# Eight moves in a fused two-branch kernel: a fold's evictions, two scaled tiles of C, half-tiles of the state, and three loads

## The chip, the cores and the metric

The kernel runs on one core of one Trainium2 chip. The core has five engines that run their own instruction streams in order and meet at semaphores: PE (TensorE, the matmuls; its weight loads are shown as PEld), DVE (VectorE), ACT (ScalarE), POOL (GpSimd, used here almost only to issue transfers that add to their target) and SP (SyncE, which issues the other transfers). The metric is device time in microseconds (us) of one execution. A profile of one execution gives, for every instruction, start, duration and what ended the wait before it. All times below count from the start of that profiled span.

## The reference

The inputs are a sequence x of 2048 rows by 1024 channels, and the weights of two branches whose results are mixed row by row with a gate g:

```python
g = _sigmoid((x * gate_w).sum(-1, keepdims=True))
a = _A_ref(x, ...)      # diagonal complex state space model
b = _B_ref(x, k, v, ...)  # gated long convolution
return g * a + (1 - g) * b
```

Branch a keeps 1024 complex states. With `Lam_bar = exp(dt * Lam)` and `B_bar = ((Lam_bar - 1) / Lam) * B` it computes `Bu = x B_bar^T`, runs `h = Lam_bar * h + Bu[t]` over all 2048 rows, and gives `y = 2 Re(h C^T) + x * Dskip`. Branch b filters k with four taps per channel, multiplies by v to get kv, convolves kv over the sequence with a kernel `ssm_k` of full length 2048 per channel (in the reference by an FFT of length 4096), adds `kv * ssm_D`, and multiplies by q, which is x itself here. Types are bfloat16 in and out.

## The kernel before

The kernel is written as one long function in which every engine's instructions are issued in the order of the code (helper `put`, line 92: all compute goes through it, which is why nearly every row of the profile is at L94). Python generators stand for pieces of work; `step(gen)` issues the piece up to the next `yield`, `run(gen)` the rest. So the order of `step` and `run` calls is a schedule written out by hand, and moving one call moves instructions on several engines at once. PSUM is one pool of four 4 KB tiles (`ps2`, line 86); a matmul group can begin only when one of the four has been evicted by ACT or DVE.

The work has three stages.

**Start (to about 60 us).** Angles of a table are reduced on DVE and turned into cosines and sines on ACT: `SF` and `CF` for the forward transform, then `SI` and `CI` for the inverse one from `inverse_angles` (line 360: two ACTIVATEs `h<-row`, then two DVE instructions) and `inverse_table`. `first_times_v` (line 537) makes the first channel block's taps, multiplies them by v and mirrors them (`ev`, `ks`). `fold_K(c)` (line 462) folds the long kernel of block c: ten matmuls into two PSUM tiles `foldk`, each evicted by ACT into `eok`. `fwd_K` and `fwd_V` multiply by the tables; their PSUM tiles are `psk` and `psv`.

**Convolution (the loop at line 1070 over c = 0 to 6, and the block after it for c = 7).** Channels go in 8 blocks of 128. In an iteration the engines work on different blocks: `inverse(c - 1)` (line 677) multiplies the product spectrum G by CI and SI (tiles `psz`, 8 matmuls each, evicted into `cv` and stored to DRAM by SP), `times_v` on block c + 1, `products(c)` (line 625) on DVE, which ends with G, and `fwd_K`, `fwd_V` of block c + 1. Between them stand `step(parts)`: a third of a tile of the state branch's Bu. `Bu_tile` (line 774) has three steps: 16 matmuls into `odd` with its eviction into U, 16 matmuls into `even`, and 8 short matmuls `even<-U,lamd` with the eviction `U<-even`. Between the second and the third step the `even` tile stays in PSUM. The input of a later part of the state branch, block 2 of x (`xT`, loaded by SP with a transposing transfer), goes into the memory that v2 holds, so that its load waits for the last `ks<-ks,v` on DVE.

**State branch (line 1188 on).** `Bu_plain` gives tiles `both` (16 matmuls, two evictions). `turn_C(pi)` (line 1199) multiplies the complex tile pi of C by a complex factor per state: two ACTIVATEs write `m`, two more multiplications scale the tile in place, and `m` is added, for pi 0, 1, 4 and 5 by a POOL transfer that adds (`gather`), for the others by DVE. `turn_U` (line 815) makes ACT write Q and POOL add it to U. Then a loop over j = 0 to 15 runs one DVE scan per j (`scan`, line 834), and matmuls `Bu_next` or `psy` (`Cy_row`, `Cy_group`) as `plan` says (line 1308: for j = 3 it is "B12 B13 C0"). `scale_b(t)` (line 941) is two ACTIVATEs on the convolution's row t (`pbb`, read back from DRAM) and on D times the gate (`gd<-rows`), and a POOL transfer that adds them. For scans 4, 12, 13 and 14 the products `Q<-hb,lam` are made by ACT when the list `put_off` is called, and DVE adds them to U in the next scan. `scale_a` evicts a `psy` tile, `combine` adds to it, `store` writes rows out.

Of the kernel before, what the change touches and what calls it, by code (L numbers as in the profile page):

```python
# [9 lines left out]
ALU = mybir.AluOpType  # L10
# [10 lines left out]
def kernel(  # L21
# [440 lines left out]
    def fold_K(c):  # L462

        kb = lds.pop(("kn", c)).rearrange("p (a f) d -> p a f d", f=4)
        eo = eos["k", c] = eo_pool.tile([128, 2, 2, 4, 128], BF16, name="eok")
        for mt in range(2):
            ps = ps2([128, 2, 4, 128], "foldk")
            for e in range(2):
                mm(ps[:, e], ident, kb[:, :, 2 + mt], True, False)
                mm(ps[:, e], refl[:, e], kb[:, :, 1 - mt], False, mt == 0)  # L470
                if mt == 1:

                    mm(ps[:, e, 0], refl[0:1, e], sD[:, c * 128:(c + 1) * 128], False, True)
            act(eo[:, :, mt], ps, func=ACT.Copy)
            yield
# [355 lines left out]
    put_off = []  # L831
# [175 lines left out]
    def step(gen):  # L1007
        next(gen, None)

    def run(gen):  # L1010
        for _ in gen:
            pass

    def steps(gen, n):
        for _ in range(n):
            step(gen)
# [12 lines left out]
    act(flat(CF), flat(hf), func=ACT.Sin, bias=pih, scale=-TWO_PI)  # L1029
    angles = inverse_angles()  # L1030
    turns = inverse_table()
    step(angles)
    step(first)
    step(first)
    run(fold_K(0))
    ts(NCF, CF, -1.0, None, ALU.mult)
    step(angles)
    run(first)
    run(angles)
    load("kT", 1)  # L1040
# [29 lines left out]
    for c in range(NC - 1):  # L1070
# [38 lines left out]
        tabs, back, prod = turn_table(c - 1) if c <= NG else none, inverse(c - 1), products(c)  # L1109
        step(old)  # L1110
        step(tabs)
        step(back)
        step(tv)
        steps(prod, 3)
# [4 lines left out]
        run(old)  # L1119
        if nn < NC:  # L1120
            dg = dgs(nn)
        if c in (2, 6):
            step(parts)
        fwd_K(n, (0, 1))
        if c in (2, 6):
# [48 lines left out]
            run(next(tiles))  # L1174
            run(next(tiles))
        fwd_V(n, (0, 1))
        if c < 6:
            step(parts)
            if c in (1, 3):
                step(parts)  # L1180
        fwd_V(n, (2, 3))
        if c == 5:
            step(parts)
        if c == 1:
            lam_diag(1, lam_pool)
# [13 lines left out]
    def turn_C(pi):  # L1199
        by_sum = pi in (0, 1, 4, 5)  # L1200
        if pi in (4, 5):
            m = [s5p["Q"].tile([128, D], BF16, name="Q") for c in range(2)]
        else:
            whole_m = m_pool.tile([128, 2, D], BF16, name="m")
            m = [whole_m[:, c] for c in range(2)]
        for c in range(2):
            act(m[c], CT[pi][:, 1 - c], func=ACT.Identity, scale=mc2i[:, pi:pi + 1])
            yield
        for c, f in enumerate((c2r, mc2r)):
            ts(CT[pi][:, c], CT[pi][:, c], f[:, pi:pi + 1], None, ALU.mult)  # L1210
            if by_sum:
                gather(CT[pi][:, c], m[c])
        if not by_sum:
            tt(CT[pi], CT[pi], whole_m, ALU.add)
# [7 lines left out]
    with tc.tile_pool(name="fin", bufs=1, side="right") as fin:  # L1222

        count = iter(range(16))

        def room(shape, dt, name):
            return fin.tile(shape, dt, name=name, tag=f"fin{next(count)}")

        prod, back = products(c, 0, room, False), inverse(c - 1)
        run(old)  # L1230
        steps(prod, 3)
        run(next(tiles))
        steps(turning[0], 2)
        step(back)
        steps(turning[1], 2)
        run(back)
        gate(1)
        gate(2)
        steps(prod, 2)
        b6, b7 = Bu(6)  # L1240
        run(b6)
        run(b7)
        s5p["Q"] = s5p["wu"]
        step(turns_U[6])
        run(turning[0])
        run(turning[1])
        run(prod)
        run(turns_U[6])
        steps(turning[2], 2)
        b8, b9 = Bu(7)  # L1250
        run(b8)
        run(b9)
        b10, b11 = Bu(8)
        run(b10)
    back = inverse(c)
    step(back)
    run(back)
    h3.close()
    wk = pool("wk", 5)
    s5p["hb"] = pool("hb", 7)  # L1260
# [8 lines left out]
    CT_pool(range(4, NP), "ctb")  # L1269
    load_CT(4)  # L1270
    load_CT(5)
    load_xT(3)
    loads(0)
    move(rows_, bc(A_Dskip.rearrange("(o d) -> o d", o=1), [128, D]))
    load_CT(6)
    loads(1)
    load_CT(7)
    loads(2)
    late = []
    on_act = []  # L1280
# [17 lines left out]
    def Cy(tb, tl):  # L1298
        ps = ps2([128, 2, 512], "psy")
        for g in range(NG):  # L1300
            Cy_g(tb, tl, [ps[:, 0], ps[:, 1]], g, g == NG - 1)
            if g == 1:
# [8 lines left out]
    turned[0] = 7  # L1311
    multiplied = {3: (0,), 4: (1,), 5: (2,), 6: (3,), 8: (4,), 9: (5,), 10: (6, 7), 11: (8,), 12: (9, 10)}
    loaded = {7: (7, 8), 8: (9, 10), 9: (11, 12), 10: (13,), 11: (14,), 12: (15,)}
    scaled_b = {1: (0,), 2: (1, 2), 5: (4,), 6: (5,), 8: (7, 8), 9: (9, 10), 10: (11,),
                11: (12, 13), 12: (14,), 13: (15,)}
    stored = {11: range(4, 8), 14: range(8, 12)}

# [26 lines left out]
    def Cy_group(tb, g):  # L1344
        if g == 0:
            end_late()
            four[tb] = [ps2([128, 2, 512], "psy") for tl in range(4)]
        for tl in range(4):
            ps, k = four[tb][tl], tb * 4 + tl
            Cy_g(tb, tl, [ps[:, 0], ps[:, 1]], g, g == NG - 1)  # L1350
            if g == NG - 1:
                scale_a(k, [(slice(0, D), flat(ps))])
                combine(k)
                if tb == 2 and tl == 1:
                    put_off[-1][0]()

    step(scans[0])
    for j in range(NS):
# [24 lines left out]
        if j == 4:  # L1383
            put_off[-1][0]()
            scale_b(3)
        for unit in plan[j].split():
            if unit[0] == "G":
                Cy_group(int(unit[1]), int(unit[2]))
            else:
                (Bu_next if unit[0] == "B" else Cy_row)(int(unit[1:]), *([[b11]] if unit == "B8" else []))  # L1390
# [63 lines left out]
```

## Time and profile before

| | |
|---|---|
| runs | 392.3, 392.07, 390.45 us (median 392.07) |
| profiled execution | 391.13 us, of which the profile's span is 389.4 us |
| granted TensorE clock | 0.998 |
| PE busy | 373.8 us in 2411 instructions |
| DVE busy | 372.4 us in 606 |
| ACT busy | 289.0 us in 442 |
| POOL busy | 76.7 us in 101 |
| transfers | 70.72 MB, mean 182 GB/s |

How to read the profile's rows below. A row of the timeline has start and duration in us, then engine, line, operation, `out<-in` by the program's names (buffer numbers left out), shapes, how many equal instructions it merges (xN), and in brackets the idle time of that engine before the row and what ended it. A row of the table of waits has who waited for whom, the sum in us, how often, and the longest. "SPq" and "POOLq" are a queue's own work; a transfer lands some us after its issue. Two PE durations overlap: consecutive 128x512 matmuls start 0.216 us apart although each is shown with 0.38 us.

### The profile page before, as it was taken

How to read it: one execution, taken by the hardware profiler on the slowest of the kernel's cores; microseconds unless marked ns; L12 is line 12 of the kernel's file. 1: busy time of each engine (PE TensorE's matmuls, PEld its weight loads, DVE VectorE, ACT ScalarE, POOL GpSimd, SP SyncE). 2: the span in 40 equal slices, each digit the busy share in tenths (PEclk: the TensorE clock that was granted, in tenths of full speed). 3: DMA queues.
4: the chain of work that ended last, by engine and by line, in shares of the span. 5: the costliest groups of instructions: out<-in, count | busy, mean ns of one | idle time of the engine just before them, and what ended most of it. 6: DMA issues, size and time to landing. Idle time of an engine off the chain costs nothing.

```text
span 389.4 us, 6580 instructions
## 1 busy us (share of the span) xinstructions
PE 373.8 (96%) x2411; PEld 196.9 (51%) x2445; DVE 372.4 (96%) x606; ACT 289.0 (74%) x442; POOL 76.7 (20%) x101
## 2 busy tenths in 40 slices
PE   8899899999999999799999999989999999999995
PEld 5366347565474756554454344434444444444442
DVE  7889999999999989999999999999999999996997
ACT  3797997978969789665674995796897868936601
POOL 3011030110302103002005010422424423535100
PEclk9999999999999999999999999999999999999999
DMA  8959999999999998588997599994998999998802
GB/s 164 163 100 240 180 224 215 214 210 176 204 185 210 238 180 174 98 162 139 184 207 152 130 185 205 238 240 91 203 224 158 230 251 220 171 246 146 196 1 108
DMA packets 135506, 70.72 MB, mean 182 GB/s; under 512 B 114921, under 2 KB 117745, under 8 KB 135474
## 3 DMA queue, kind: packets, MB, share of 16 engines
q1 hardware_dynamic: 122992, 46.16, 56.2%
q0 software_dynamic: 12400, 24.12, 36.4%
q8 instruction: 19, 0.31, 0.3%
q14 instruction: 13, 0.11, 0.1%
q10 hardware_dynamic: 82, 0.02, 0.0%
HBM read 12.86 MB, written 8.39 MB: 55 GB/s over the span
## 4 chain that ended last, share of the span: by engine, by line
PE 58%; DVE 27%; ACT 7%; issue 5%; DMA 2%; ACTq 0%; DVEq 0%; POOLq 0%
PE psy L94 20%; PE both L94 12%; PE psk L94 7%; DVE BT L94 6%; DVE wkh L94 6%; PE psz L94 4%; PE even L94 3%; DVE G L94 3%; PE psv L94 3%; PE odd L94 3%; DVE t L94 3%; PE foldk L94 2%; PE taps L94 2%; ACT Vh L94 1%; DVE W L94 1%
## 5 line engine op out<-in xcount | busy, mean ns | idle before, releaser
L94 PEld LDWEIGHTS <-BT 128*128 128x128 bf16 x640 | 61.7, 98 | 48.7 <-DMA xT<-in_A_x_dram 0.3
L94 PE MATMUL both<-xT,BT 128*128 128x512 bf16 x375 | 83.2, 379 | 0.5
L94 POOL DMA_DIRECT2D U<-Q x22 | 24.2, 1113 | 85.3 <-ACT Q L94 62.4
L94 PEld LDWEIGHTS <-hb 128*128 128x128 bf16 x256 | 24.9, 98 | 31.6 <-issue 1.8
L94 PEld LDWEIGHTS <-U 128*128 128x128 bf16 x240 | 23.5, 98 | 28.3
L94 ACT ACTIVATE Vh<-psv 128x1024 bf16<-128x1024 f32 x32 | 30.9, 1037 | 8.0 <-PE psv L94 7.9
L94 PE MATMUL psy<-CT,hb 128*128 128x512 bf16 x156 | 36.6, 379 | 0.2
L94 ACT ACTIVATE U<-both 128x512 bf16<-128x512 f32 x44 | 24.3, 594 | 15.3 <-PE both L94 15.0
L94 PE MATMUL psy<-CT,U 128*128 128x512 bf16 x149 | 34.3, 379 | 0.1
L94 DVE TENSOR_TENSOR_SCAN W<-rv,init,A 128x256 bf16<-128x256 f32 x48 | 32.2, 729 | 0.0
L94 POOL DMA_DIRECT2D G<-wkh x8 | 9.8, 1219 | 100.8 <-DVE wkh L94 100.8
L94 PE MATMUL psk<-eok,SF 128*128 128x512 bf16 (+1 forms) x119 | 27.9, 354 | 0.3
L94 PE MATMUL psz<-G,CI 128*128 128x512 bf16 x64 | 24.3, 380 | 4.1 <-DVE G L94 3.2
L94 PEld LDWEIGHTS <-SF 128*128 128x128 bf16 x184 | 18.0, 98 | 19.6 <-issue 1.1
L94 ACT ACTIVATE Q<-U,lam 128x512 bf16<-128x512 bf16 (+1 forms) x44 | 25.4, 606 | 0.0
L94 PE MATMUL psz<-G,SI 128*128 128x512 bf16 x64 | 24.2, 379 | 0.0
L94 PE MATMUL psy<-CTa,hb 128*128 128x512 bf16 x95 | 22.6, 379 | 1.4 <-ACT U L94 1.3
L94 DVE TENSOR_TENSOR wkh<-BT,Vh 128x3072 bf16<-128x3072 bf16 (+4 forms) x20 | 21.8, 1110 | 0.0
L94 PE MATMUL taps<-dg,kT 128*128 128x128 bf16 (+1 forms) x352 | 21.8, 210 | 0.0
L94 PEld LDWEIGHTS <-kT 128*128 128x128 bf16 x352 | 21.2, 100 | 0.7 <-DMA kT<-in_B_k_dram 0.2
L94 DVE TENSOR_TENSOR wkh<-Kh,Vh 128x3072 bf16<-128x3072 bf16 (+2 forms) x16 | 21.3, 1349 | 0.0
L94 PE MATMUL psy<-CTa,U 128*128 128x512 bf16 x87 | 20.4, 379 | 0.1
(217 smaller groups left out, 830.9 us busy)
## 6 DMA issues: line engine op xcount, KB each, us to landing
U<-Q POOLq DMA_DIRECT2D x22, 256.0 KB, 5.6
G<-wkh POOLq DMA_DIRECT2D x6, 768.0 KB, 9.0
cv_scr<-cv SPq DMA_DIRECT2D x16, 256.0 KB, 4.3
v<-in_B_v_dram SPq DMA_DIRECT2D x5, 512.0 KB, 6.9
out_dram<-m SPq DMA_DIRECT2D x8, 256.0 KB, 5.3
BT<-cv_scr SPq DMA_DIRECT2D x7, 256.0 KB, 9.6
out_dram<-BT SPq DMA_DIRECT2D x7, 256.0 KB, 2.9
ks<-lo POOLq DMA_DIRECT2D x6, 256.0 KB, 8.2
```

The source lines that it names most:

```text
L94: i = f(*a, **kw)
```

## The change

Eight edits, none of which adds or removes a matmul or a transfer:

- (a) In the start, `step(angles)` moves from before `first` and `fold_K(0)` to behind them: on ACT the two `eok<-foldk` come ahead of the two `h<-row`, and on DVE `ev` and `ks` come ahead of `rq<-h`.
- (b) In iteration c = 4 the third step of a state tile (8 short matmuls and `U<-even`) moves from between the second and third `psv` tile to behind the fourth.
- (c) In iteration c = 6 the second step of a state tile (16 matmuls `even<-xT,BT`) moves from behind `inverse(5)` to ahead of it.
- (d) The in-place scaling of C's tiles 0 and 1 (four instructions of 128x1024) goes from DVE to ACT.
- (e) `run(turning[0])` moves ahead of `turn_U[6]`, and the two ACTIVATEs `m<-CTa` of tile 2 move from ahead of `Bu(7)` to behind `inverse(7)`.
- (f) On SP's queue, row 0's two loads and the load of D come ahead of the two transposed loads of x's block 3, and C's tile 7 ahead of row 1's loads.
- (g) `scale_b(2)` moves from j = 2 to j = 3, behind the matmuls B12 and B13 and ahead of C0.
- (h) The products `Q<-hb,lam` of scan 12 move from between the second and third of four `psy` evictions to ahead of the first.

```diff
@@ -1029,12 +1029,11 @@
     turns = inverse_table()
-    step(angles)
     step(first)
     step(first)
     run(fold_K(0))
+    step(angles)
     ts(NCF, CF, -1.0, None, ALU.mult)
-    step(angles)
     run(first)
     run(angles)
@@ -1109,6 +1108,8 @@
         step(old)
         step(tabs)
+        if c == 6:
+            step(parts)
         step(back)
@@ -1119,7 +1120,7 @@
-        if c in (2, 6):
+        if c == 2:
             step(parts)
         fwd_K(n, (0, 1))
@@ -1174,12 +1175,12 @@
         fwd_V(n, (0, 1))
-        if c < 6:
+        if c < 6 and c != 4:
             step(parts)
             if c in (1, 3):
                 step(parts)
         fwd_V(n, (2, 3))
-        if c == 5:
+        if c in (4, 5):
             step(parts)
@@ -1207,7 +1208,10 @@
         for c, f in enumerate((c2r, mc2r)):
-            ts(CT[pi][:, c], CT[pi][:, c], f[:, pi:pi + 1], None, ALU.mult)
+            if pi < 2:
+                act(CT[pi][:, c], CT[pi][:, c], func=ACT.Identity, scale=f[:, pi:pi + 1])
+            else:
+                ts(CT[pi][:, c], CT[pi][:, c], f[:, pi:pi + 1], None, ALU.mult)
             if by_sum:
                 gather(CT[pi][:, c], m[c])
@@ -1240,13 +1244,12 @@
         run(b6)
         run(b7)
+        run(turning[0])
         s5p["Q"] = s5p["wu"]
         step(turns_U[6])
-        run(turning[0])
         run(turning[1])
         run(prod)
         run(turns_U[6])
-        steps(turning[2], 2)
         b8, b9 = Bu(7)
@@ -1255,6 +1258,7 @@
     back = inverse(c)
     step(back)
     run(back)
+    steps(turning[2], 2)
     h3.close()
@@ -1269,12 +1273,12 @@
     load_CT(4)
     load_CT(5)
-    load_xT(3)
     loads(0)
     move(rows_, bc(A_Dskip.rearrange("(o d) -> o d", o=1), [128, D]))
+    load_xT(3)
     load_CT(6)
+    load_CT(7)
     loads(1)
-    load_CT(7)
     loads(2)
@@ -1311,7 +1315,7 @@
-    scaled_b = {1: (0,), 2: (1, 2), 5: (4,), 6: (5,), 8: (7, 8), 9: (9, 10), 10: (11,),
+    scaled_b = {1: (0,), 2: (1,), 5: (4,), 6: (5,), 8: (7, 8), 9: (9, 10), 10: (11,),
                 11: (12, 13), 12: (14,), 13: (15,)}
@@ -1349,10 +1353,10 @@
             if g == NG - 1:
+                if tb == 2 and tl == 0:
+                    put_off[-1][0]()
                 scale_a(k, [(slice(0, D), flat(ps))])
                 combine(k)
-                if tb == 2 and tl == 1:
-                    put_off[-1][0]()
@@ -1384,6 +1388,8 @@
         for unit in plan[j].split():
+            if unit == "C0":
+                scale_b(2)
             if unit[0] == "G":
```

## The prediction

> **What bounds the kernel now.** I read the page's engine shares first, then the waits of PE and DVE, then the timelines around each wait.
>
> ```profile
> PE 373.8 (96%) x2411; PEld 196.9 (51%) x2445; DVE 372.4 (96%) x606; ACT 289.0 (74%) x442; POOL 76.7 (20%) x101
> ```
>
> ```profile
> PE psz L94 <- DVE G L94: 3.2, 2, 1.8
> PE psk L94 <- ACT eok L94: 1.8, 2, 1.2
> PE psy L94 <- ACT U L94: 1.3, 1, 1.3
> ...
> PE psz L94 <- ACT U L94: 0.4, 1, 0.4
> ...
> DVE U L94 <- ACT Q L94: 3.8, 2, 3.2
> DVE G L94 <- ACT Vh L94: 3.3, 3, 2.2
> ```
>
> PE and DVE are both nearly full and hand the bound to each other, so time can come only from the few waits, and a wait removed on one engine counts only as far as the other is early too. The places, by the timelines of PE, ACT, DVE, POOL and SP:
>
> ```profile
> 14.88 0.38 PE L94 MATMUL psk<-eok,CF 128*128 128x512 bf16 x1 [0.53 <-ACT eok L94]
> ...
> 165.21 0.39 PE L94 MATMUL psz<-G,CI 128*128 128x512 bf16 x1 [1.84 <-DVE G L94]
> ...
> 259.26 2.75 PE L94 MATMUL psy<-CTa,hb 128*128 128x512 bf16 x12 [1.28 <-ACT U L94]
> ```
>
> ```profile
> 11.51 1.50 ACT L94 ACTIVATE h<-row,colat,colneg 128x512 f32<-128x512 f16 x2
> 12.91 1.91 ACT L94 ACTIVATE eok<-foldk 128x1024 bf16<-128x1024 f32 x2
> ...
> 214.64 2.19 ACT L94 ACTIVATE m<-CTa,mc2i 128x1024 bf16<-128x1024 bf16 x2 [5.37 <-issue]
> ```
>
> ```profile
> 356.02 0.69 DVE L94 TENSOR_TENSOR U<-U,Q 128x1024 bf16<-128x1024 bf16 x1 [3.23 <-ACT Q L94]
> ```
>
> ```profile
> 175.32 0.36 POOL L94 COPY stamp<-xT 128x2 bf16<-128x2 bf16 x1 [19.80 <-DMA xT<-in_A_x_dram]
> ```
>
> ```profile
> 166.31 4.41 SPq L94 DMA_TRANSPOSE xT<-in_A_x_dram  x2
> ```
>
> The reader sees PE waiting for late evictions (14.88, 259.26) and for DVE (165.21), ACT blocked 5.37 us by tile 2's `m` while finished `both` tiles wait in PSUM, DVE waiting 3.23 us for ACT near the end, and x's block 2 landing at 175.2.
>
> **Part by part.** Minus is earlier, against the profiled execution; landings of transfers are the completions that the trace records for them.
>
> (a) The first fold is evicted at 11.5 instead of 12.91; the second waits for its matmuls (end 12.4) and ends at 13.5 instead of 14.82. PE's `psk` starts at 13.5: −1.4. The two `h` (1.50) now run until 14.9, just when the first `psk` tile is ready (16.33 − 1.4). On DVE `ev`, `ks` (2.4) go first and `rq` waits for `h`, to 17.0 instead of 17.17, where the taps' diagonals are needed by 18.0 (19.41 − 1.4). DVE's own wait at 20.77 (2.18, for Vh) shrinks with PE and ACT. So all three carry −1.4. The loads behind (SP's chain from 25.74 on) are released by taps and `ks<-ks,v`, so they move along. Cover: the taps of block 3 start at 61.25 and their last transfer lands at 60.9; both move. If the transfers do not, up to 1.4 is lost.
>
> (b) DVE waits 0.94 at 142.71 for four Vh; ACT runs them from 138.42 with one `U<-even` (0.48) between. Without it: DVE −0.5, in all −1.9. Pinning `even` over two more `psv` leaves three PSUM tiles; the fourth `psv` (139.9) needs the first Vh, evicted at 139.4: nothing. `ks<-lo`, 0.2 late at 157.9, lands earlier as DVE does: PE −1.6.
>
> (c) PE is free at 163.2 and G comes at 165.2, after (b) at 163.3. The 16 `even` matmuls (169.10 to 170.85: 1.75) fill 161.6 to 163.35, so `psz` goes out at −1.9 and the work behind the inverse at −3.6. Of the PSUM tiles `even` now pins one during `psz`, mirror, `psz`, `psk`, `psk`; each next tile's eviction (168.1, 169.0, 170.2) is 0.7 us or more before its need at 169.1, 170.0, 171.3: nothing, at most the 1.6 us that PE would wait for two evictions. But the next `both` (175.64) needs x's block 2. Its load is issued when DVE ends `ks<-ks,v` (166.29), so it lands at 175.2 − 1.9 = 173.3, and PE, there at 172.0, waits 1.3: −2.3 from here on.
>
> (d) DVE loses four rows of 0.40 each, start to start (208.11 to 209.69): −1.6 on its way to G, which is ready at 215.75 − 1.9 − 1.6 = 212.3. PE arrives at 215.2 − 2.3 = 212.9, so G no longer delays it (0.6). ACT gains four ACTIVATEs; the nearest row is `m<-CTa` of the same shape, 1.05 start to start (2.19 for two), the dearest `pbb<-pbb`, also in place, 1.15: 4.2 to 4.6, I take 4.2. They lie in the 5.37 that ACT was blocked. The Trainium skill, "ScalarE: Activation LUTs", section Rules for kernel authors, says the opposite of this edit: multiplications belong on VectorE, up to about three times faster in bf16. The rows agree on the price (0.40 against 1.05); by the rule the sum would lose 2.6 us, by the trace's idle ACT nothing.
>
> (e) ACT no longer stands before tile 2's `m` (whose buffer comes free at 214.57): after its last U at 204.1 (206.4 − 2.3) it has 4.2 us of scaling and 2.9 of Q, evicts the three `both` from 211.3 to 214.6, and PSUM is free when the second `psz` needs it at 214.7. PE's second hole (217.57 to 218.11) goes: −0.5, so `both` at 219.83 becomes 216.4 (−3.45). `m` runs behind `cv`, to 219.6; DVE wants it at 225.33 − 3.5 = 221.9: 2.3 us of cover, beyond which DVE pays one for one. POOL issues tile 0's two sums before U's first, which DVE needs at 221.5; it has 8 us.
>
> (f, g) In j = 1 to 3 ACT waits 1.19 and 1.77 for row 0 and D, 1.98 for tile 7 of C, and does rows 1 and 2 before B12's evictions, so `psy` starts 1.47 late (PE free at 257.79, start 259.26). Loads first and row 2 later: ACT reaches B12's evictions at about 252, PE needs the tile at 254.3. The 1.47 go: −4.9. x's block 3 is moved behind three issues of 1.5 us but its queue starts 4.6 earlier (it waited for `cv`); it landed at 238.6, needed at 244.0. Row 2's sum is issued 1 us later and lands near 264; DVE wants it at 267.
>
> (h) ACT is idle from 344.6 to 351.93, and hb of scan 12 is ready at 348.8; the four Q take 2.55, so they are done at 351.4, before DVE wants them at 352.8: DVE's 3.23 + 0.53 go, −3.5 − 3.7 = −7.2. PE never waited there. The four evictions wait at most 0.7 behind Q (the first tile is ready at 347.3, with (a) to (g) taken off, and Q ends at 348.0), with 3 us until their PSUM is reused. So the end passes to PE: its last matmul ends at 384.7, but DVE read the last half at 385.84, being 1.1 behind. Now DVE is waiting: −4.9 − 1.1 = −6.0.
>
> Sum along PE: 1.4 + 0.9 (b and c, capped by block 2) + 1.1 (d, e) + 1.5 (f, g) + 1.1 (h) = 6.0. The profiled execution took 391.13 (span 389.4 and 1.7 around it): 385.1. The median of the runs is 0.9 above it: **386.1**.
>
> **The rivals.**
> - Transfers do not follow: block 2 lands at 175.2 as before, because issue and landing are set by the queue. PE then has −0.4 at 175.64 (its slack there) instead of −2.3 and waits until G hides nothing: 1.9 lost, 388.0. If (a)'s 1.4 goes too, 389.4. For: 9 us from issue to landing; 1.07 mean DMA share from 46 to 142 us. Against: the issue waits for DVE, visibly.
> - ScalarE becomes the bound, part by part: Q, C and evictions late by 1 to 3 us between 203 and 255, so 0.6 to 1.5 stay: 387 to 388. For: ACT 37.7 of 44 busy from 215 to 259.
> - The waits only move and the sum is nothing: the known holes of PE refill with other waits; 392. Against: five separate places.
> - Slower: `m` of tile 2, now behind `cv`, comes late and DVE's first scan stalls, pushing all 16. Place 221.9, cover 2.3; each further us costs one, on a DVE that is 1.2 earlier than PE at the end. From 2.3 + 1.2 + 6.0 = 9.5 us late it decides; ten us late gives 393, twelve 395. Only `cv` and `psz`, themselves tied to PE, precede it; nothing shows such a delay.
>
> **How the numbers follow.** Forecast 0.55 (384.5 to 387); transfers 0.16 (to 389.4); ScalarE 0.14; nothing changes 0.07; slower 0.08. No change means within 0.5%, 2 us, about what these runs tell apart. The range reaches from 384.3 (DVE's −7.2 plus a run below the median) to 390.6, leaving the last two cases and some of the edges out. The first three are faster: 0.85; same 0.07; slower 0.08.
>
> **What would show it.** Right: the holes at 14, 165, 216, 218 and 259 gone, a new PE wait near 173 of about 1.3 for x's block 2; no DVE wait for Q near 349; the last chain on PE, not DVE, from 354 on. Wrong: a PE wait for evictions near 214 or 252 (ACT late), a landing of block 2 later than 174, a DVE wait at `CTa<-CTa,m` near 222.

## The result, and the profile after

The changed kernel takes 389.23 us in the median of 14 runs beside 391.47 for the kernel before on the same chip: a ratio of 0.9933, 95% interval 0.9909 to 0.9957. Timed a second time beside the experiments it gave 0.993 (0.9903 to 0.9957). So it is faster by 0.7%, where the forecast was 1.5% (385.1 for a profiled execution of 391.13). The direction is right and the median lies in the range, but the size is less than half: −2.2 us between the medians instead of −6.0. The profiled execution took 387.75 with a span of 386.0: −3.4 instead of −6.0. Two of the changed kernel's runs, 393.15 and 393.71, count as slow and are left out of the ratio; the other twelve spread from 386.51 to 391.02 (median 388.73), those of the kernel before from 390.4 to 392.42. The spread is part of the story.

Engine shares, first part of the page, and the engine line of the chain that ended last, of the changed kernel:

```profile
PE 373.6 (97%) x2411; PEld 197.4 (51%) x2445; DVE 371.3 (96%) x602; ACT 292.2 (76%) x446; POOL 77.1 (20%) x101
...
DVE 23%; DMA 14%; issue 8%; SPq 3%; ACT 3%; PE 2%; POOL 1%; DVEq 0%; POOLq 0%; ACTq 0%
```

DVE and PE are as full as before. The shares of the chain cannot be set beside those before (PE 58%, DVE 27%, transfers 2%): in this execution the view follows the chain only back to 175.10, and the shares add up to 54% of the span. In a second execution of the same kernel PE has 46% of the chain and DVE 43%. The waits of PE and DVE (who, for whom, sum, times, longest):

```profile
PE both L94 <- DMA xT<-in_A_x_dram: 2.3, 2, 1.6
PE psz L94 <- DVE G L94: 1.3, 1, 1.3
...
DVE xr L94 <- PE both L94: 2.7, 1, 2.7
```

The waits for `eok`, for evictions at psy and for Q are gone or small (`eok` 0.4), as forecast. Two are new: PE's for x's blocks 2 and 3, of which the first was forecast, and 2.7 us of DVE at `xr`. The timelines at these places, PE, ACT, DVE, POOL, then SP's queue:

```profile
13.78 0.38 PE L94 MATMUL psk<-eok,CF 128*128 128x512 bf16 x1 [0.36 <-ACT eok L94]
...
174.05 1.24 PE L94 MATMUL both<-xT,BT 128*128 128x512 bf16 x4 [1.57 <-DMA xT<-in_A_x_dram]
...
242.16 1.02 PE L94 MATMUL both<-xT,BT 128*128 128x512 bf16 x4 [0.74 <-DMA xT<-in_A_x_dram]
...
255.97 1.24 PE L94 MATMUL psy<-CTa,hb 128*128 128x512 bf16 x5
...
217.29 0.22 ACT L94 ACTIVATE U<-ends 128x4 bf16<-128x4 bf16 x1 [3.01 <-DMA U<-Q]
...
238.99 1.15 ACT L94 ACTIVATE Q<-CT,mc2i 128x1024 bf16<-128x1024 bf16 x1 [4.82 <-DMA U<-Q]
...
249.88 0.69 DVE L94 TENSOR_TENSOR xr<-xr,pbb 128x1024 bf16<-128x1024 bf16 x1 [2.74 <-PE both L94]
...
353.10 1.19 DVE L94 TENSOR_TENSOR U<-U,Q 128x1024 bf16<-128x1024 bf16 x2
...
229.34 0.86 POOL L94 DMA_DIRECT2D U<-Q  x1 [4.45 <-DMA U<-Q]
...
244.94 0.90 POOL L94 DMA_DIRECT2D pbb<-gd  x1 [14.75 <-DMA CT<-in_A_C_im_dram]
...
229.18 10.49 SPq L94 DMA_TRANSPOSE xT<-in_A_x_dram  x2
```

`xr<-xr,pbb` is row 0's product (`product(0)`), which reads the sum `pbb<-gd` that POOL issued at 244.94. By the completions that the trace records, this sum landed at 249.80, just ahead of 249.88; the releaser that the page names ("PE both") is the wrong one. In each of the ten traces, this one and nine of the experiments', in which DVE waits over 1 us for row 0's product, it starts 0.08 us after that sum's landing. The same views of the kernel before, for DVE, POOL and SP's queue:

```profile
249.66 0.68 DVE L94 TENSOR_TENSOR xr<-xr,pbb 128x1024 bf16<-128x1024 bf16 x1
...
228.83 0.86 POOL L94 DMA_DIRECT2D U<-Q  x1 [4.14 <-ACT U L94]
...
244.22 0.86 POOL L94 DMA_DIRECT2D pbb<-gd  x1 [14.54 <-ACT U L94]
...
229.43 7.07 SPq L94 DMA_TRANSPOSE xT<-in_A_x_dram  x2
```

Up to 217 us DVE gained 2.9 us (its first scan at 214.87 instead of 217.74) and PE 2.7. Then nothing in the stretch of the moved loads came earlier any more: ScalarE waits 3.01 at 217, so that `cv` and SP's loads begin only 1.9 earlier. The second U sum of tile 7 is issued at 229.34, half a microsecond later than before, and takes 9.6 us (landing at 238.96) instead of 4.5. ScalarE, whose next Q goes into the buffer that this sum reads, waits 4.82 for it; row 0's sum is therefore issued at 244.94 instead of 244.22; and DVE waits until 249.88, where it had been at 249.66 before the change without any wait. At scan 6 it is 0.4 us behind the kernel before. What is left at the end is PE's −3.3.

### The profile page after: what moved, and what is told of

It is laid out like the page before. It is cut to its first block, busy times and chain, and to the rows that moved or that the text cites. A ratio compares the mean times of both kernels' runs of the same rounds, so it can differ in the third digit from the quotient of the medians.

```text
span 386.0 us, 6577 instructions
## 1 busy us (share of the span) xinstructions
PE 373.6 (97%) x2411; PEld 197.4 (51%) x2445; DVE 371.3 (96%) x602; ACT 292.2 (76%) x446; POOL 77.1 (20%) x101
## 4 chain that ended last, share of the span: by engine, by line
DVE 23%; DMA 14%; issue 8%; SPq 3%; ACT 3%; PE 2%; POOL 1%; DVEq 0%; POOLq 0%; ACTq 0%
DMA U<-Q 7%; DVE W L94 4%; SPq L94 3%; DVE G L94 3%; DVE hb L94 3%; DMA xT<-in_A_x_dram 2%; DVE t L94 2%; DMA out_dram<-m 2%; DVE A L94 2%; PE both L94 2%; DVE trn L94 2%; DMA G<-wkh 2%; DVE wkh L94 1%; DVE U L94 1%; DMA m<-xr 1%
## 5 line engine op out<-in xcount | busy, mean ns | idle before, releaser
L94 ACT ACTIVATE U<-both 128x512 bf16<-128x512 f32 x44 | 24.2, 594 | 14.1 <-PE both L94 13.9
L94 POOL DMA_DIRECT2D U<-Q x22 | 23.3, 1072 | 57.6 <-ACT Q L94 26.5
```

Source lines behind the costliest of these rows:

```text
L94: i = f(*a, **kw)
```

## The experiments

Theory T, after this reading: the loads that (f) puts in front, and the U sum among them, make row 0's sum late, and VectorE's lead dies there. Rivals: ScalarE's own order, (d) and (e), does it; or (h) alone is what was gained.

**The same kernel again, and one edit undone or moved at a time.**

> The changed kernel once more, for a second trace and for times on the same chip as the next three. Theory T (transfers): the second U sum of tile 7 is issued within 0.2 us of the two transposed loads of x's block 3 (229.34 and 229.18 in the first trace), so which of them is served first differs from run to run; where the sum lands late, ScalarE waits about 5 us for its buffer near 239, row 0's sum comes late and VectorE waits up to 3 us at row 0's product; where it lands within 5 us, these waits shrink below 1 us and the run is 1 to 2 us shorter. Time 386.5 to 391, median 389 +- 0.7. Rival R (compute order): the waits are set by the order of ScalarE's own work, and recur within 0.3 us of 3.01, 4.82 and 2.74 whatever the run's time is.

Measured 388.36 (ratio 0.993). The waits were 3.05, 4.09 and 2.64, the second U sum took 9.0 us. They recur, two of the three within the rival's 0.3 and the second 0.7 shorter; on this the rival is nearer: the race between the sum and block 3's load was lost in both traces. That the order of ScalarE's own work sets these waits, as the rival has it, does not follow, and the next runs speak against it. What differed was the start (below).

```diff
+    load_xT(3)
     loads(0)
     move(rows_, bc(A_Dskip.rearrange("(o d) -> o d", o=1), [128, D]))
-    load_xT(3)
     load_CT(6)
-    load_CT(7)
     loads(1)
+    load_CT(7)
```

> The changed kernel with edit (f) undone: x's block 3 loads first again, C's tile 7 behind row 1. Theory T: the loads put in front are what delays the second U sum and block 3. Block 3 is issued near 227 and lands by 237 (PE's wait of 0.74 goes), the sum lands within 6 us of its issue, ScalarE's wait of 4.82 falls below 1.5, VectorE's wait at row 0's product falls below 0.5, ScalarE waits again 1 to 2 us for row 0 and D as before the change; PE's first psy starts within 0.5 us of the changed kernel's. Time 1 to 2 us below the changed kernel on the same chip (about 387.5 in the median, ratio to before 0.989). A variant of T in which the transposes themselves hold the sum up: the sum still lands 8 us or more after its issue and the time stays within 0.5 of the changed kernel. Rival R: nothing changes in VectorE's wait (2.5 to 3), and the time is as the changed kernel's or, with the wait for the psy tiles back, 1 us above it.

Ratio 0.9919 (0.9888 to 0.9951), 387.64, not told apart from the changed kernel. The timelines of this run for ACT, DVE and PE:

```profile
234.96 1.15 ACT L94 ACTIVATE Q<-CT,mc2i 128x1024 bf16<-128x1024 bf16 x1 [0.95 <-DMA U<-Q]
...
250.44 1.15 ACT L94 ACTIVATE m<-CT,mc2i 128x1024 bf16<-128x1024 bf16 x1 [4.12 <-DVE A L94]
...
249.37 0.69 DVE L94 TENSOR_TENSOR xr<-xr,pbb 128x1024 bf16<-128x1024 bf16 x1 [2.46 <-issue]
...
257.20 1.02 PE L94 MATMUL psy<-CTa,hb 128*128 128x512 bf16 x4 [2.17 <-ACT U L94]
```

Half of theory T holds: with block 3 first, the U sum takes 4.8 us and block 3 lands at 237.5; ScalarE's 4.82 becomes 0.95. The other half fell: DVE's wait at the product stays (2.46), because row 0's sum, issued 2.8 us earlier, took 7.2 us and landed at 249.29 all the same. And the stall goes round: ScalarE waits 4.12 for DVE ahead of C's tile 7, and PE 2.17 for the evictions behind that.

```diff
     def between(j):
-        for k in multiplied.get(j, ()):
-            product(k)
+        if j != 3:
+            for k in multiplied.get(j, ()):
+                product(k)
         yield
         if j == 3:
             run(turning[6])
+            product(0)
```

> The changed kernel with row 0's product moved on VectorE from ahead of scan 3's recurrences to behind them (about 4 us later); nothing else moves. It takes away what waits for row 0's late sum, not the late sum. Theory T: VectorE's wait of 2.74 falls to below 0.5, VectorE reaches scan 12 about 2.5 us earlier, and the end passes to PE, which is then 1.1 us less far ahead of it: 1.1 us below the changed kernel (about 388.1 in the median), no more, because PE has only its own -3.3. Rival R2 (VectorE's lead would have been lost at a later place anyway, by the U sums between 270 and 320): VectorE waits the same 2 to 3 us later and the time stays within 0.4 us of the changed kernel.

Ratio 0.9937 (0.9904 to 0.9969): no gain. In the traced execution (392.28) everything was late: the U sum took 12.0 us, row 0's sum landed at 255.33, and DVE waited 1.27 even behind the scan. The expected gain of 1.1 is refuted as a median; moving what waits does not help while the sum itself can be this late. (Two stretches of PE at half rate, behind its waits at 173.55 and 245.27 and of the kind shown in the last section, made this execution late too.)

```diff
+                scale_a(k, [(slice(0, D), flat(ps))])
+                combine(k)
-                if tb == 2 and tl == 0:
+                if tb == 2 and tl == 1:
                     put_off[-1][0]()
-                scale_a(k, [(slice(0, D), flat(ps))])
-                combine(k)
```

> The changed kernel with edit (h) undone: Q of scan 12 again between the second and third of the four evictions. The prediction counted 1.1 us at the end for (h) and let VectorE's 3.23 + 0.53 go by it. Theory T: where VectorE has lost its lead at row 0's product, (h) gives nothing, because PE is 3.3 us earlier and brings the evictions and with them Q to about 352.7, when VectorE is there at 353.1: within 0.4 us of the changed kernel. Rival R3 (what was measured is (h) alone and the moves ahead of it gave nothing): the wait of over 3 us for Q is back and the time is that of the kernel before, 391.5.

Ratio 0.9942 (0.9917 to 0.9966): as the changed kernel. DVE's timeline in this run:

```profile
354.16 0.66 DVE L94 TENSOR_TENSOR U<-U,Q 128x1024 bf16<-128x1024 bf16 x1
355.19 0.76 DVE L94 TENSOR_TENSOR U<-U,Q 128x512 bf16<-128x512 bf16 x2 [0.37 <-ACT Q L94]
```

Of the 3.23 + 0.53 that DVE waited for Q before the change, 0.37 is left without (h). DVE is late and PE, which brings the evictions ahead of Q, is early; so they meet. Rival R3 is refuted: (h) is not what was gained.

**Where the sum loses its time.**

```diff
-        run(turning[0])
         s5p["Q"] = s5p["wu"]
-        step(turns_U[6])
+        run(turns_U[6])
+        run(turning[0])
         run(turning[1])
         run(prod)
-        run(turns_U[6])
```

> The changed kernel with the whole of turn_U of tile 6 (six ACTIVATEs into Q and the two POOL sums into U) ahead of the scaling of C's tiles 0 and 1, so that the two U sums are issued ahead of the four sums into CTa. Theory T1 (the wait of 3.0 that ScalarE has at 217 in every trace of the changed kernel comes from the order of POOL's sums, and everything behind it, cv, its stores, SP's loads and row 0's sum, is late by it): the wait falls below 0.8, cv is evicted from about 216, C's tile 4 begins to load at 218.5 instead of 221.0, row 0's sum lands at 248 or earlier instead of 249.8, VectorE's wait at row 0's product falls below 1.2, PE does not wait for x's block 3. Time about 1.3 below the changed kernel (387.2 in the median). Rival B1 (the bytes in front set when row 0's sum lands, not when their issue begins): the wait of 3.0 goes, but row 0's sum lands again at 249.3 to 250.3, VectorE waits 2.5, and the time stays within 0.5 of the changed kernel.

```profile
216.98 1.02 ACT L94 ACTIVATE cv<-psz 128x1024 bf16<-128x1024 f32 x1 [0.70 <-PE psz L94]
...
238.62 1.15 ACT L94 ACTIVATE Q<-CT,mc2i 128x1024 bf16<-128x1024 bf16 x1 [6.90 <-DMA U<-Q]
...
251.12 0.69 DVE L94 TENSOR_TENSOR xr<-xr,pbb 128x1024 bf16<-128x1024 bf16 x1 [4.51 <-issue]
```

These are ACT's and DVE's rows of this run. The wait of 3.0 at 217 is gone (0.7 is left, for PE), so its cause, the place of U's sums behind those into C, is shown; C's tile 4 starts to load at 218.6. But the second U sum, issued 2.5 us earlier, lands at 238.60 as before, after 11.7 us, together with block 3's first half (238.79). Rival B1 is right about this: issuing earlier alone buys nothing; DVE's wait became longer (4.51) than either side had it. Ratio 0.9904 (0.9866 to 0.9942).

```diff
     load_CT(3)
+    move(rows_, bc(A_Dskip.rearrange("(o d) -> o d", o=1), [128, D]))
...
     loads(0)
-    move(rows_, bc(A_Dskip.rearrange("(o d) -> o d", o=1), [128, D]))
     load_xT(3)
```

> The changed kernel with the load of D (256 KB) issued behind C's tile 3, near 190, instead of behind row 0's loads at 228.7: one transfer less in front of x's block 3 and the second U sum. Theory B1 (bytes): what stood behind it lands about 1 us earlier: the U sum by 238, block 3 by 241.2 (no PE wait), row 0's sum near 248.7 and VectorE's wait near 1.6; time 0.5 to 1 below the changed kernel. Rival T2 (the U sum is held up by the transposed loads and not by the bytes of D): the sum still takes 8 us or more, and VectorE's wait and the time change by less than 0.4.

Ratio 0.9927 (0.9901 to 0.9952). With 256 KB less in front the U sum still takes 10.6 us, block 3 lands at 242.38, and DVE waits 5.35. Rival T2 is right about the sum and the time; DVE's wait, which it had unchanged, grew by 2.6.

```diff
         ps = ps2([128, 2, 2, HB], "both")
+        if tb == 2 and "awake" not in inv:
+            inv["awake"] = True
+            for _ in range(5):
+                mm(flat(ps[:, 0]), BT[g][:, 0, 0, 0:128], flat(BT[g][:, 0, 0:2]), True, True)
```

> The changed kernel with five 128x512 matmuls more (1.08 us, their result is overwritten) at the place where PE waits 1.2 to 1.6 us for x's block 2. They compute nothing that is used; they only keep PE busy in most of that wait. Theory H (a wait of PE of over a microsecond is sometimes followed by about 3.2 us in which every 128x512 matmul takes 0.43 instead of 0.216, 1.65 us lost, as seen behind 174, 246 and 258 in three traces; this is what spreads the runs): no such stretch behind 174, the wait left is 0.2 to 0.5, the fastest runs are as before (386.5) and the median is 0.3 to 0.8 lower than the changed kernel's. Rival N (the spread comes from the start and from the transfers alone): median and spread are unchanged within 0.4, or 0.5 higher where the added matmuls delay the block.

388.97, ratio 0.9919 (0.9883 to 0.9955), runs from 386.22 up: the distribution is not told apart from the changed kernel's. No half-rate stretch followed at 174 in this trace, but most traces have none there anyway. Undecided as a cure.

The last three diffs together:

> The changed kernel with the three edits of the last three together: U sums ahead of C's scaling, D loaded early, five matmuls in the wait for block 2. If T1 and B1 hold together, row 0's sum lands near 246.5 and VectorE's wait is gone, VectorE keeps its lead of about 3 us to the end and PE sets the end: 385.5 to 386.5 in the median, the forecast's value. If only PE's own waits count, 387.5; if the row's sum is bound by bytes, 388.

388.79, ratio 0.9911 (0.9879 to 0.9944); the U sum took 7.7 us, row 0's sum landed at 252.02, DVE waited 4.09. The forecast's value did not come: with the loads in (f)'s order, neither early sums nor an early D save the lead.

**Combinations.** The first takes the edits of the first two diffs above (block 3 first, product later):

> The changed kernel with both edits of two earlier runs: (f) undone (x's block 3 loads first again) and row 0's product behind scan 3's recurrences. Theory T3 (VectorE loses its lead at row 0's product alone, whose sum lands near 249.5 whatever is loaded first; and it is this stall that makes ScalarE wait 4.1 for VectorE ahead of C's tile 7 and PE 2.2 for B12's evictions): VectorE's wait at the product is below 0.6, scan 4 starts 2 to 3 us earlier than in the kernel before (at 262.3 or earlier), ScalarE's 4.1 falls below 1.5, PE's wait at the first psy below 0.8, so that it starts by 255.8; the end moves by 4.5 to 5.5 against the kernel before, 386 to 386.6 in a run without a half-rate stretch, ratio to before 0.987. Rival (the stall only moves on, to the U sums or to ScalarE): VectorE is level with the kernel before at scan 6 again, ratio 0.992 as with (f) undone alone.

388.81, ratio 0.989 (0.9822 to 0.9958); the traced execution, 393.65, was 5 us above that median. In it the U sum took 8.3 us, DVE did not wait at row 0's product, but waited 2.10 at row 1's, ScalarE waited 4.56 for C's tile 7, and PE 3.97 at the first psy. In that execution the stall moved on; since it was so much later than the others, it decides nothing between theory and rival.

The next adds the U sums first, D early, and three matmuls near 6.3 us:

```diff
     def columns():
+        raise_clock(1)
         mm(psp[:, 0, 0:3 * ND], prow, ident[64:64 + 3 * ND, 64:64 + 3 * ND], True, True)
+        raise_clock(2)
```

> As the last one, and besides: the U sums of tile 6 ahead of C's scaling, D loaded near 190, and three 128x512 matmuls more near 6.3, where PE waits 0.2 and 0.35 for small loads and copies. Theory T3: as the last one or 0.5 to 1 better, since cv, SP's loads and row 0 begin 2.5 us earlier; ratio 0.985. Rival: transfers bind and nothing is gained over the last one; ratio as there within 0.002.

386.75, ratio 0.9854 (0.9803 to 0.9906). No wait of DVE above 0.2 us from 175 to 377, where it begins to wait for the last psy tiles; scan 6 at 280.32 (before 282.84).

The kernel before with (h) alone:

```diff
             if g == NG - 1:
+                if tb == 2 and tl == 0:
+                    put_off[-1][0]()
                 scale_a(k, [(slice(0, D), flat(ps))])
                 combine(k)
-                if tb == 2 and tl == 1:
-                    put_off[-1][0]()
```

> The kernel before with edit (h) alone. The prediction's own step: VectorE's 3.23 and 0.53 go, but the end then passes to PE, which was 1.1 ahead: -1.1, ratio 0.997. Rival L (VectorE's wait was the whole of it): -3.4, ratio 0.991, which would make (h) the whole of the measured gain. Rival Z (it gives nothing because PE brings Q late all the same): ratio 1.000 and the wait of about 3 us still there.

```profile
356.81 1.53 DVE L94 TENSOR_TENSOR U<-U,Q 128x1024 bf16<-128x1024 bf16 x3
...
386.88 1.41 DVE L94 SCALAR_TENSOR_TENSOR BT<-psy,gcols,xlast 128x512 bf16<-128x512 f32 x2 [0.42 <-PE psy L94]
...
383.23 3.62 PE L94 MATMUL psy<-CT,U 128*128 128x512 bf16 x16
```

Ratio 0.9983 (0.9949 to 1.0017): nothing that can be told from no change. DVE's and PE's rows show why the prediction's 1.1 was too much. Both waits for Q are gone (a wait of 2.01 for a later row's sum, at 349.73, is new) and the end has passed to PE; DVE now waits 0.42 for it. But DVE ends 1.45 us after PE's last matmul here (388.30 − 386.85), and before the change it ended 1.80 after it (386.50 − 384.70). Passing the end from DVE to PE is worth 0.35, not 1.1. The same 1.44 or 1.45 ends each trace in which DVE waits for PE there.

The changed kernel with only the three matmuls at the start:

> The changed kernel with three 128x512 matmuls more (their result is not used) around the small ones near 6.3 us, so that PE does not idle there. In four of nine traces of changed kernels the 48 taps behind this place ran at half rate (4.5 instead of 2.85 us) and edit (a) then had nothing to take, because the fold's evictions waited for PE. Theory W (that stretch follows from PE's little work between 6.2 and 7.1): the taps run in 2.85 us plus at most 0.3 in this trace, the first psk is at 13.1 to 13.4, and the median falls by 0.3 to 0.6 below the changed kernel's (ratio 0.992). Rival V (it comes from how the run's start falls and not from PE's idling): the stretch can be there again, and the median does not change or rises by 0.3, the added work.

389.64, ratio 0.9941 (0.9912 to 0.997): no gain. The taps ran at full rate in this trace and in the five others with these matmuls, as they did in two thirds of the traces without them; six traces are too few to call that a cure.

**Which pair is enough.** The combination again, and with one part put back each: in the second the order of loads (the diff), in the third `product(0)` ahead of the `yield` in `between`, in the fourth the two steps of `turns_U[6]` among C's scaling.

```diff
     load_CT(5)
-    load_xT(3)
     loads(0)
+    load_xT(3)
     load_CT(6)
+    load_CT(7)
     loads(1)
-    load_CT(7)
```

> The version with five edits on the changed kernel (block 3 first, D loaded near 190, U sums ahead of C's scaling, row 0's product later, three matmuls more near 6.3) once more, beside the next three. If its 386.75 (ratio 0.985) was no accident of six runs: 386.3 to 387.5 in the median, ratio 0.984 to 0.989, VectorE 2 us or more ahead of the kernel before from scan 4 to scan 12, no wait of PE at the first psy. If it was: 388 to 389.

> That version with edit (f)'s order of loads back (row 0 ahead of x's block 3, C's tile 7 ahead of row 1); D stays early. Theory F (the order of (f) itself eats the gain: a U sum and the transposed loads of block 3 then overlap and both slow down): the second U sum of tile 7 takes 8 us or more from issue to landing, block 3 lands behind 239.5, row 0's sum behind 248.5, and the time is 0.8 to 1.5 above the version's. Rival G (the order of loads is indifferent once the sums come early and the product late): within 0.4 of the version.

> That version with row 0's product back ahead of scan 3's recurrences. VectorE reaches it near 246.8, row 0's sum landed there at 246.8: by theory F the loads' order alone saves the lead, a wait below 0.7 and a time within 0.4 of the version's; by rival P (the product's place is what counts) a wait of 2 to 3 and a time 1 us above it.

> That version with the U sums of tile 6 among C's sums again, as the change has them. ScalarE's wait of 3.0 near 217 is back, cv and everything behind it 1.5 us later. By theory T1 (that wait delays the loads and through them row 0's sum) the sum lands near 248.5 and the time is 0.4 to 0.8 above the version's; by rival G it is within 0.3.

Ratios 0.9894 (0.9862 to 0.9926), 0.9881 (0.985 to 0.9912), 0.9852 (0.9826 to 0.9879), 0.9878 (0.9855 to 0.9901). The repetition lies between its two forecasts. Neither product nor sums are needed one by one, and rows first did not cost the 0.8 expected where the product stands later: of theory F's landings none came (U sum 7.1 us, block 3 at 237.10, row 0's sum at 247.78), nor did T1's in the fourth (row 0's sum at 245.62). By time rival G is right in both. The third, with the product in its old place, beats both kernels (386.28 in the median; its interval lies below the changed kernel's). Its shares, and DVE's, PE's and ACT's rows at the places of the second fence of timelines:

```profile
PE 376.1 (98%) x2448; PEld 197.4 (51%) x2448; DVE 371.3 (96%) x602; ACT 293.3 (76%) x446; POOL 77.7 (20%) x101
```

```profile
246.98 0.68 DVE L94 TENSOR_TENSOR xr<-xr,pbb 128x1024 bf16<-128x1024 bf16 x1
...
350.19 1.53 DVE L94 TENSOR_TENSOR U<-U,Q 128x1024 bf16<-128x1024 bf16 x3
...
255.27 1.03 PE L94 MATMUL psy<-CTa,hb 128*128 128x512 bf16 x4
...
217.49 1.02 ACT L94 ACTIVATE cv<-psz 128x1024 bf16<-128x1024 f32 x1 [0.70 <-PE psz L94]
```

Row 0's product starts at 246.98 without a wait (row 0's sum landed at 244.85), 2.7 us ahead of the kernel before, and DVE reaches `U<-U,Q` at 350.19 instead of 356.02. The execution took 386.8; DVE ends 4.35 earlier.

Two more leave parts out: the changed kernel with the first diff (block 3 first) and D early, and with the first diff and the U sums first.

> The changed kernel with block 3 loaded first again (edit (f) undone) and D loaded near 190, nothing else. Theory F2 (what keeps VectorE's lead is that x's block 3 and D both leave the way of row 0's sum; the other edits of the combinations are not needed): row 0's sum lands by 246.5, VectorE's wait at the product is below 0.7, VectorE is 2 us or more ahead of the kernel before at scan 6, ratio 0.984 to 0.990. Rival S (POOL's sums must come early as well): the sum lands near 248, a wait of 1 to 2, VectorE level with the kernel before, ratio 0.991 to 0.993.

> The changed kernel with block 3 loaded first again and the U sums of tile 6 ahead of C's scaling; D stays behind row 0's loads. Theory F2: ScalarE waits for D again (0.5 to 1.5), row 0's sum lands at 247.5 to 249, VectorE's wait is 1 to 2.5, ratio 0.990 to 0.993. Rival S: the sum lands by 246.5, the wait is below 0.7, ratio 0.984 to 0.990, so that D's place is indifferent.

Ratios 0.9908 (0.9872 to 0.9944) and 0.989 (0.9847 to 0.9933). In neither trace did DVE wait at the product. In the second, rival S's signs came: row 0's sum landed at 246.36. The first trace (390.01) was late for other reasons: PE waited at 108.8, and ran at half rate behind block 2's wait. Its scan 2 starts at 240.61, no earlier than before the change (239.88), so that DVE had no lead there to lose, and it can't show that D alone is enough. By time neither is told from the changed kernel.

Times alone don't separate the neighbours, landings do. The table gives, by the completions in each trace, how long the second U sum of tile 7 took, and when row 0's sum landed, counted from the start of scan 2, against which a trace's own delay drops out as far as it delays compute and transfers alike. VectorE can begin the product 9.8 us after that start. Each row without "two traces" is one trace.

| loads | besides (on the changed kernel) | U sum took | row 0's sum after scan 2 | DVE's wait | ratio |
|---|---|---|---|---|---|
| rows first | nothing, two traces | 9.6, 9.0 | 12.6, 12.4 | 2.74, 2.64 | 0.9933, 0.993 |
| rows first | (h) undone | 9.1 | 12.4 | 2.64 | 0.9942 |
| rows first | matmuls at the start | 7.8 | 12.8 | 2.91 | 0.9941 |
| rows first | matmuls at block 2 | 7.8 | 13.0 | 3.17 | 0.9919 |
| rows first | product later | 12.0 | 16.9 | 1.27, later | 0.9937 |
| rows first | sums first | 11.7 | 14.3 | 4.51 | 0.9904 |
| rows first | D early | 10.6 | 15.1 | 5.35 | 0.9927 |
| rows first | sums first, D early, matmuls at block 2 | 7.7 | 13.9 | 4.09 | 0.9911 |
| rows first | sums first, D early, product later, start | 7.1 | 11.4 | none, later | 0.9881 |
| block 3 first | nothing | 4.8 | 12.3 | 2.46 | 0.9919 |
| block 3 first | product later | 8.3 | 13.9 | none at row 0 | 0.989 |
| block 3 first | D early | 5.3 | 9.0 | none | 0.9908 |
| block 3 first | sums first | 4.8 | 8.6 | none | 0.989 |
| block 3 first | D early, product later, start | 5.1 | 8.4 | none | 0.9878 |
| block 3 first | sums first, D early, start | 5.0 | 7.7 | none | 0.9852 |
| block 3 first | all five, two traces | 4.7, 5.1 | 9.7, 8.5 | none | 0.9854, 0.9894 |
| block 3 first | kernel before; with (h) | 4.5, 5.3 | 9.5, 9.7 | none | 1, 0.9983 |

With rows first the U sum took 7.1 to 12.0 us and row 0's sum missed the 9.8 each time. With block 3 first it took 4.5 to 5.3, one late trace of 8.3 apart, and the row's sum made the 9.8 in each trace in which D, the U sums or both were out of its way too (for D alone with the doubt named above). So (f)'s order of loads is the part that has to be undone for VectorE to keep its lead at the product's old place, but undoing it is not enough by itself: 12.3 and 13.9 without the other edits. That this is because the compute around it has moved up by 2.8 us and the transfers have not is argued, not shown. That the U sum and the transposed loads slow each other while they overlap is what the landings suggest: in seven of the ten traces with rows first the sum lands within 0.7 us of block 3's first half, having started beside it. What holds them inside the transfer engines no view here shows, and it stays open.

## Why the prediction was right and wrong

- **(a) right, a little large.** −1.10 at `psk` (13.78) instead of −1.4: the fold now waits for its load, which landed 0.26 later in this execution. The gain has a condition that the prediction did not see. In four of the twelve traces that have (a) and no added matmuls at the start, PE ran the 48 taps ahead of the fold at half rate, and the first psz came within 0.22 us of that in the trace of the kernel before, whose taps ran at full rate.
- **(b) right.** DVE's G at 141.06 instead of 142.71, −1.65 with (a)'s −1.1; its wait fell from 0.94 to 0.39.
- **(c) right in kind.** PE does psz at 163.66 without a wait and is stopped by block 2: issued 1.65 earlier, landed at 173.91 instead of 175.18. −1.6 at `both` instead of −2.3. So block 2's rival, "transfers do not follow", was wrong; it followed by 1.3 of 1.65. What the prediction left out is that the new wait of PE can be followed by a half-rate stretch (below): in 2 of the 16 traces that have this wait and no added matmuls in it.
- **(d) right in price.** DVE gained about what its four rows cost: its `G<-G,wkh` behind them starts at 206.82 instead of 209.69 (−2.87), where at 197.55, ahead of them, it was 1.41 early; 1.46 for the 1.6. The four ACTIVATEs start 1.04 us apart, as priced. The rule that the prediction drew from the Trainium skill, "ScalarE: Activation LUTs", section Rules for kernel authors (multiplications on VectorE), did not decide: moving them to ScalarE was no loss here, by the trace; no run undoes (d) alone.
- **(e) half right.** Both holes at psz(7) are gone and `both` starts at 217.09 instead of 219.83: −2.7, −3.45 said. The cover of tile 2's `m` held: it ended at 222.5, DVE came at 223.60 with no wait. The failing words are "POOL issues tile 0's two sums before U's first, which DVE needs at 221.5; it has 8 us". DVE had the time, but ScalarE needed the memory that the second U sum reads, and waited 3.01: the sum landed at 217.26, ScalarE went on at 217.29. The sums-first run shows this as the cause.
- **(f, g) is the step that failed: what the moved loads do to the sums in flight was priced at nothing.** "x's block 3 is moved behind three issues of 1.5 us but its queue starts 4.6 earlier": the queue started 1.9 earlier, because of that 3.01. And three transfers were priced by their issue instead of by what they do to others in flight: block 3's two loads took 10.5 us on the queue instead of 7.1, the U sum 9.6 instead of 4.5. PE's hole at 259.26 did go (psy at 255.97 with no wait), but 0.74 came back at block 3, so that 0.55 of the 1.5 was left there; and DVE's lead of 2.7 died at row 0's product, at which the prediction had not looked at all: it had no wait before.
- **(h) mis-sized.** The term "1.1 (end passes from DVE to PE)" measures 0.35 where the end passes. In the changed kernel, where DVE has lost its lead, the end does not pass, and (h) is worth nothing that was measured.

The sum, by its own terms: PE came to −3.3 instead of −4.9 (0.3 less in (a), 0.4 at block 2, 0.74 at block 3, and 0.15), and the last 1.1 did not come, since DVE and not PE set the end. With row 0's sum in time, the trace of the best version has PE at −4.0 and the end at −4.35, and the five traces of the combinations with the three matmuls at the start end at −4.35 to −5.4. So of the missing 2.6, 0.75 was the wrong size at the tail, 0.3 the fold's load in (a) and 0.4 block 2's landing; the rest, about 1.1, was lost to transfers between 217 and 250, and 0.95 of it is back in the best version's trace. This split is an estimate from single traces.

Among the rivals, "ScalarE becomes the bound" gave 387 to 388, and the profiled execution took 387.75. Its number fits and its mechanism does not: ScalarE waited 7.8 us in that stretch for sums to land, it did not run out of time. "The waits only move" was right for DVE's lead, which was gone by scan 6, and wrong for PE. The slower rival's place, tile 2's `m`, stayed covered.

## What to carry to other kernels

When everything ahead of a stretch gets earlier, look up each transfer's landing in it, and not only the waits that exist: the next stall stands where a landing had slack of a few tenths (row 0's sum landed 0.3 ahead of its use) and no wait showed. Price a load that is moved forward by the bytes and transposes it will share the engines with, and follow which compute engine needs the memory that a transfer still reads. And a lead of one engine counts only if nothing on its way is tied to transfers; check the last landing before the end of the stretch first.

## What the runs showed of the hardware that was not expected

**A short wait of PE can be followed by a halved clock.** Two stretches of the run with the product moved, and the one before, from the view by windows of time (us, then busy time of PE, PEld, DVE, ACT, POOL, the granted clock, transfers' share, GB/s):

```profile
170.00:173.50 3.50, 2.23 (x39) 1.43 (x37) 3.50 (x14) 3.48 (x5) 0.00 (x0) 1.00 1.24 173
...
174.20:177.30 3.10, 3.10 (x9) 1.13 (x8) 3.10 (x4) 0.12 (x2) 2.01 (x2) 0.50 0.53 94
177.30:181.00 3.70, 3.70 (x18) 1.66 (x17) 3.70 (x5) 1.18 (x3) 0.00 (x0) 0.97 1.07 186
```

PE had waited 1.33 us for block 2. Then it got half its clock, by the trace's record of the clock from 174.13 to 177.55: 9 matmuls in 3.1 us where the next 3.7 us hold 18, each 0.43 apart instead of 0.216, about 1.65 us lost. By the starts of the matmuls, all traces together have 52 idle stretches of PE of 0.8 us or more later than 16 us, and six were followed by this: four of the five longer than 2.1 us, two of the other 47. So it is chance at 1.5 us and likely above 2, it adds 1.5 us or more where it hits, and it is one source of the spread from 386.5 to 391.

The records of the clock show where the chance comes from, at least in part. From the first grant of the full clock to the last drop, behind the end of PE's work, each stretch at full or half clock in every trace is a whole multiple of 3.413 us long (at half clock 3.413 in five places and twice that in one). So the clock changes on a grid, and a wait can fall inside one piece of it or across an edge. Cut along this grid, by an estimate from the matmuls' starts, the four pieces in which PE had least work, 5 to 37% of a piece, were all followed by half clock; of the 28 with 38 to 59% two were.

The Trainium skill, "TensorE: Matmul & The Clock Gate", section "HAM oscillation — how this bites in real kernels", asks for no idle gap above about 3.4 us; here five waits from 1.33 to 2.65 us were enough (the sixth was 3.97), so the measurement is stricter than the Trainium skill, and it decides. The Trainium skill, "TensorE: Matmul & The Clock Gate", section "Part 1: The HAM clock gate", says that the window by which the clock is set runs freely, which agrees with the same wait being punished in some traces only.

**The same at the start, where the column does not show it.** The taps of block 0 in two traces of the same kernel, the first fence the first trace:

```profile
7.27 2.85 PE L94 MATMUL taps<-dg,kT 128*128 128x128 bf16 x48
```

```profile
7.10 4.45 PE L94 MATMUL taps<-dg,kT 128*128 128x128 bf16 x48
```

The granted clock is printed as 1.00 in both. That the second took 1.6 us more for the same 48 matmuls is seen in the durations, and in when the trace's record of the clock begins: the first grant of the full clock stands at 10.35 to 10.93 us in the four traces with slow taps and at 4.71 to 6.88 in the other sixteen. Before its first record the column shows 1.00 all the same.

**Sums and loads share more than an issue queue.** The Trainium skill, "DMA: Bandwidth & Descriptors", section "Issuing engines are not separate DMA queues", says that transfers of all issuers run interleaved on the same engines. The traces agree in so far as a sum's time depends on what SP loads beside it, and put a price on it: 4.5 to 5.3 us for a 256 KB sum beside one order of loads (8.3 in one late trace), 7.1 to 12.0 beside the other.
